# The last product of a decode layer turned from four rows into four columns, with the output stored from 128 partitions

## The chip, the cores and the metric

The kernel runs on one core of a Trainium2 chip, as one launch. The metric is the device time of one execution in microseconds; the kernel before takes 355.39 us, the median of three runs (355.38 to 355.53). Engine names in the profile: PE is TensorE (PEld its weight loads), DVE is VectorE, ACT is ScalarE, POOL is GpSimd, SP is SyncE, which here only issues DMAs.

## The reference

One decode step of a conditioned transformer block, for a single token with D = 512. The condition c gives six vectors of 512 (shift, scale and gate for each half). The first half is attention with 32 query heads over 8 cached key and value heads of 32768 positions; the second half is a feed-forward layer with 1792 hidden units.

```python
mod = (_silu(c) @ w_mod).reshape(c.shape[0], 6, 1, -1)
sa, ca, ga, sb, cb, gb = (mod[:, i] for i in range(6))
h = _layernorm(x) * (1 + ca) + sa
x = x + ga * attention(h, k_cache, v_cache, wq, wo)      # 8 heads x 32768 x 128, keys and values
h = _layernorm(x) * (1 + cb) + sb
x = x + gb * (relu(h @ w1) @ w2)                          # 512 -> 1792 -> 512
```

Everything is bf16 in memory. The key and value caches are 64 MB each, and the weights some 16 MB; all of it is read once.

## The kernel before

**Loads.** All large loads are issued from SP in one fixed order (`stream`, L139 to L144; `load` and `need`, L96 to L151): w_mod, wq, then keys and values in pieces of 4 MB, then wo in four pieces, w1 in two and w2 in six. They go into a ring of five slots of 32 KB per partition (L74); a load waits until the slot that it takes is free. w2 is held as 14 rows of 512 per partition, so `w2_sb[p, ft, d]` is the weight from hidden unit 14p + ft to output d. Its six pieces hold ft = 0 to 3, 4 to 6, 7 to 9, 10 and 11, 12, and 13 (`W2P`, L51).

**Column form and row form.** A vector of 512 in column form lies on 128 partitions, four elements each: element 4p + ko at partition p, column ko. x, the modulation vectors (`modT_sb`) and the residual after attention (`x1T`) are held like that. In row form it lies on four partitions, 128 elements each. `expand` and `four_rows` (L323 to L337) turn columns into four rows: the column form is multiplied into a masked 128x128 tile on VectorE, and a matmul with `rowpick` sums it into four rows of PSUM. The kernel does this for the last gate in the setup (`gb_rows`, L340) and for the residual during the second layer norm (`meanwhile`, L698, and L707).

**Order.** In the setup a scheduler orders the instructions. From L599 on, TensorE and VectorE run their instructions as written: for each of 8 heads keys are turned on VectorE (L405), scores are made on TensorE (L422), then softmax and the value product (L484). After the last head the tail is serial: the rest of the output projection (`project`, L555, of which the last two pieces use wo as the stationary operand and one column as the moving one, L567), gate and residual (L691, L692), the second layer norm (L250 to L280), the w1 product (L714), Relu and the w2 product. `keep_clock(n)` (L592) issues n matmuls whose result nobody reads, in places where TensorE would otherwise have nothing to do.

**The end of the tail.** The hidden vector is transposed on VectorE in two halves (L724), and ScalarE writes its Relu into `hid_bd`, a tile of 14 x 4 x 4 columns that was zeroed in the setup and of which only the diagonal of each 4x4 block is written. So the stationary operand `hid_bd[:, ft, i, :]` has one column that is not zero, column i, and the product with 128 columns of w2 adds to row i of a 4x128 tile in PSUM. There are 14 x 4 = 56 such matmuls (L735). Two VectorE operations on 4 partitions apply gate and residual (L740, L742), and SP stores four runs of 256 bytes (L743).

PSUM tiles that go by `bank` (L240) rotate over three banks; a new one takes the bank that was used three before.

Of the kernel before, what the change touches and what calls it, by code (L numbers as in the profile page):

```python
# [9 lines left out]
BF16 = mybir.dt.bfloat16  # L10
F32 = mybir.dt.float32
ACT = mybir.ActivationFunctionType
ALU = mybir.AluOpType
AX = mybir.AxisListType
# [3 lines left out]
def kernel(  # L18
# [14 lines left out]
    nc = tc.nc  # L33
    P = 128
# [4 lines left out]
    KT = D // P  # L39
    Dff = B_w1.shape[1]  # L40
    FT = Dff // P
# [33 lines left out]
    const = ctx.enter_context(tc.tile_pool(name="const", bufs=1))  # L75
# [85 lines left out]
    ident_f = const.tile([P, P], F32)  # L161
# [7 lines left out]
    for hp in range(4):  # L169
# [10 lines left out]
        out=mask4, in_=ident_f[:].rearrange("p (x q) -> p q x", q=REP), op=ALU.add, axis=AX.X,  # L180
# [3 lines left out]
    for n in sorted({n * REP for _, n in WOP}):  # L184
        cmask[n] = const.tile([P, P // n], F32, name=f"cmask{n}")
        nc.vector.tensor_reduce(
            out=cmask[n][:], in_=ident_f[:].rearrange("p (c r) -> p c r", r=n), op=ALU.add, axis=AX.X,
# [3 lines left out]
            out=rsel_f[:], in_=ident_f[:].rearrange("p (c r) -> p r c", r=n), op=ALU.add, axis=AX.X,  # L191
# [13 lines left out]
    place32 = const.tile([P, 32], F32)  # L205
    nc.vector.tensor_reduce(
        out=place32[:], in_=ident_f[:].rearrange("p (j m) -> p m j", m=32), op=ALU.add, axis=AX.X,
    )
    rowpick = const.tile([P, KT], F32)
    nc.vector.tensor_reduce(  # L210
        out=rowpick[:], in_=ident_f[:].rearrange("p (j m) -> p j m", m=32), op=ALU.add, axis=AX.X,
    )
    hid_bd = const.tile([P, FT, KT, KT], BF16)
    nc.gpsimd.memset(hid_bd[:], 0.0)

    pick8 = const.tile([16, 8], BF16)
    nc.vector.tensor_tensor(out=pick8[:], in0=ident_bf[0:16, 0:8], in1=ident_bf[0:16, 8:16], op=ALU.add)
# [22 lines left out]
    def bank(name):  # L240
        return ps_s.tile([P, 512], F32, tag="s", name=name)[:]
# [75 lines left out]
    for i in range(2):  # L317
# [1 line left out]
            mod_rows[:, i, :].rearrange("q (m ko) -> q ko m", ko=KT),  # L319
            modT_sb[:, 4 * KT * i:4 * KT * (i + 1)].rearrange("p (j ko) -> p j ko", j=4),  # L320
        )

    def expand(src_T, name):  # L323
        e = const.tile([P, 32, KT], F32, name=f"{name}_exp")
        nc.vector.tensor_tensor(
            out=e[:], in0=src_T.unsqueeze(1).to_broadcast([P, 32, KT]),
            in1=place32[:].unsqueeze(2).to_broadcast([P, 32, KT]), op=ALU.mult,
        )
        return e

    def four_rows(e, name):

        r_ps = bank(f"{name}_ps")[0:KT, 0:P]
        nc.tensor.matmul(  # L334
            r_ps, lhsT=rowpick[:], rhs=e[:].rearrange("p m kt -> p (m kt)"), start=True, stop=True,
        )
        return r_ps  # L337

    gb_rows = const.tile([KT, P], F32)
    nc.scalar.copy(out=gb_rows[:], in_=four_rows(expand(modT_sb[:, 5 * KT:6 * KT], "gb"), "gb"))  # L340

    hT = const.tile([P, KT], BF16)
    stat1 = const.tile([P, 2], F32)
# [5 lines left out]
    ncb = const.tile([P, KT], F32)  # L349
# [242 lines left out]
    def keep_clock(n):  # L592

        if not spare:
            spare.append(bank("spare_ps"))
        for _ in range(n):
            nc.tensor.matmul(spare[0], lhsT=ident_bf[:], rhs=qbd[0][:, :, 0:P], start=True, stop=True)  # L597

    with tc.manual_schedule(engines={mybir.EngineType.PE, mybir.EngineType.DVE}):  # L599
        build_qbd(0)  # L600
        for u in range(NTILE):
            for half in range(2):
                turn_k(0, u, half)
                scores(0, u, half)
            if u % 2 == 1:
                bank_max(0, u // 2)
        soft = softmax(0)
        for _ in soft:
            pass
        soft = None  # L610
        for g in range(LAST):
            h = g + 1
            build_qbd(h)
            turn_k(h, 0, 0)
            turn_k(h, 0, 1)
            turn_k(h, 1, 0)
            scores(h, 0, 0)
            if soft:
                next(soft)
            open_o(g)  # L620
            scores(h, 0, 1)
            if soft:
                next(soft)
            if g > 0:
                blocks(g - 1)
            scores(h, 1, 0)
            if g > 0:
                o_cols(g - 1)
            turn_k(h, 1, 1)
            scores(h, 1, 1)  # L630
            if soft:
                next(soft)
            if g > 0:
                normalise(g - 1)
                if g in [sum(w) for w in WOP]:
                    spread(part_of(g - 1))
            if soft:
                next(soft)
            bank_max(h, 0)
            next(soft or iter(()), None)  # L640
            pv(g, (0, 1))
            for u in (2, 3):
                for half in range(2):
                    turn_k(h, u, half)
                    scores(h, u, half)
            bank_max(h, 1)
            soft = softmax(h)
            next(soft)
            if g < LOOPED:
                pv(g, (2, 3))  # L650
                next(soft)
                continue
            next(soft)
            next(soft)
            pv(g, (2,), range(6))
            next(soft)
            next(soft)
            open_o(LAST)
            pv(g, (2,), range(6, 16))
            pv(g, (3,))  # L660
            next(soft)
            next(soft, None)
            a_rows.append(row_bank("a_ps"))
            blocks(g)
        pv(LAST, (0, 1))
        o_cols(LAST - 1)
        normalise(LAST - 1)
        pv(LAST, (2,))
        spread(2)
        hid_ps = ps_o.tile([P, 512], F32, tag="o", name="hid_ps")  # L670
        nc.vector.memset(hid_ps[:], 0.0)
        pv(LAST, (3,))
        blocks(LAST)
        project(0)
        keep_clock(2)
        o_cols(LAST)
        keep_clock(2)
        project(1)
        normalise(LAST)
        spread(3)  # L680
        keep_clock(2)
        project(2)
        keep_clock(1)
        join_rows()
        keep_clock(2)
        project(3)


        stat2 = const.tile([P, 2], F32)
        x1T = const.tile([P, KT], F32)  # L690
        nc.vector.tensor_tensor(out=x1T[:], in0=attnT_ps, in1=modT_sb[:, 2 * KT:3 * KT], op=ALU.mult)  # L691
        nc.vector.scalar_tensor_tensor(  # L692
            out=x1T[:], in0=x1T[:], scalar=1.0, in1=xT, op0=ALU.mult, op1=ALU.add, accum_out=stat2[:, 0:1],
        )
        h2T = const.tile([P, KT], BF16)
        x1_ps = []

        def meanwhile():  # L698
            e = expand(x1T[:], "x1")
            keep_clock(2)  # L700
            x1_ps.append(four_rows(e, "x1"))
            keep_clock(2)

        keep_clock(3)
        layernorm_T(x1T[:], stat2, h2T[:], modT_sb[:, 3 * KT:4 * KT], ncb[:], "ln2", meanwhile)
        x1_rows = const.tile([KT, P], F32)
        nc.vector.tensor_copy(out=x1_rows[:], in_=x1_ps[0])  # L707

        NQ = 32 * FT
        for part, (k0, k1) in enumerate(W1P):  # L710
            w1_sb = need(("w1", part))
            for kt in range(k0, k1):
                for q in range(4):
                    nc.tensor.matmul(  # L714
                        hid_ps[32 * q:32 * q + 1, 0:NQ], lhsT=h2T[:, kt:kt + 1],
                        rhs=w1_sb[:, kt - k0, q * NQ:(q + 1) * NQ], start=False, stop=(kt == KT - 1),
                        skip_group_check=True,
                    )
        keep_clock(3)
        hidT = rows_sb("hidT").rearrange("p a b -> p (a b)")[:, 0:NQ].rearrange("p (f e) -> p f e", e=32)  # L720
        hid_v = hid_ps[:, 0:NQ].rearrange("p (e f) -> p f e", f=FT)
        hb = hid_bd[:]
        for f0, f1 in ((0, FT // 2), (FT // 2, FT)):
            nc.vector.transpose(out=hidT[:, f0:f1], in_=hid_v[:, f0:f1])  # L724
            nc.scalar.activation(
                out=AP(hb.tensor, hb.offset + KT * KT * f0, [hb.ap[0], [KT * KT, f1 - f0], [KT + 1, KT]]),
                in_=hidT[:, f0:f1, 0:1].to_broadcast([P, f1 - f0, KT]), func=ACT.Relu,
            )

        ffn_ps = bank("ffn_ps")[0:KT, 0:P]  # L730
        for part, (f0, f1) in enumerate(W2P):
            w2_sb = need(("w2", part))
            for ft in range(f0, f1):
                for i in range(KT):
                    nc.tensor.matmul(  # L735
                        ffn_ps, lhsT=hid_bd[:, ft, i, :], rhs=w2_sb[:, ft - f0, i * P:(i + 1) * P],
                        start=(ft == 0 and i == 0), stop=(ft == FT - 1 and i == KT - 1),
                    )
        o_rows = const.tile([KT, P], F32)
        nc.vector.tensor_tensor(out=o_rows[:], in0=ffn_ps, in1=gb_rows[:], op=ALU.mult)  # L740
        o_bf = const.tile([KT, P], BF16)
        nc.vector.tensor_tensor(out=o_bf[:], in0=o_rows[:], in1=x1_rows[:], op=ALU.add)  # L742
    nc.sync.dma_start(out=out[0, 0].rearrange("(i n) -> i n", i=KT), in_=o_bf[:])  # L743


# [28 lines left out]
```

## Time and profile before

| what | value |
|---|---|
| median of three runs | 355.39 us |
| the profiled execution's own time | 355.74 us |
| its span, first to last instruction | 353.9 us |
| TensorE busy | 279.8 us, 79% of the span |
| VectorE busy | 203.1 us, 57% |
| HBM read | 149.42 MB, 422 GB/s over the span |
| DMA packets | 6852, of which 824 under 512 B |
| mean granted TensorE clock | 0.947 |
| w1 product (L714) | starts at 346.09 us |
| w2 product (L735), 56 matmuls | 347.89 to 351.18 us |
| issue of the store (L743) | 351.84 us |

Times inside the execution are microseconds from the start of the span. A row of the timeline merges instructions of one kind: start, length, engine, line, operation, output and inputs with their shapes, how many (x), and in square brackets how long the engine was idle before and what ended it. "128*4 128x128" in a matmul row is the stationary operand's shape and the moving operand's. Matmuls and weight loads overlap in the engine's pipeline, so the duration of one (a mean in ns) is longer than the distance from one to the next; the distance comes from the length of a merged row and its count.

### The profile page before, as it was taken

The page shows a single profiled execution, that of the slowest core. Times are in us where ns is not written, and L with a number is a line of the kernel's source. Part 1 is how long each engine was busy: PE and PEld are TensorE (multiplying, and loading weights), DVE is VectorE, ACT ScalarE, POOL GpSimd, SP SyncE. Part 2 cuts the span into 40 slices and gives each one's busy share as a digit, 9 for nine tenths or more (in the row PEclk, how much of TensorE's full clock was granted, in tenths as well). Part 3 has the DMA queues.
Part 4 walks back from the last instruction along what each step waited for, and adds up shares of the span by engine and source line. Part 5 has one row for each costly group of instructions (what it writes and reads, how often), then busy time and mean ns, then how long its engine had stood idle before and what let it go on. Part 6 is the DMA issues. An engine that isn't in the chain of part 4 may idle for free. (4 is left out here: it accounts for less than half of the span.)

```text
span 353.9 us, 4006 instructions
## 1 busy us (share of the span) xinstructions
PE 279.8 (79%) x1311; PEld 112.7 (32%) x1311; DVE 203.1 (57%) x271; ACT 25.4 (7%) x69; POOL 3.9 (1%) x16
## 2 busy tenths in 40 slices
PE   0542781999898979897979796979689687989996
PEld 0221230333343323332323232323234233334444
DVE  6245775882768268462939178553938095734142
ACT  1220003000010001000100001000100010002000
POOL 4000000000000000000000000000000000000000
PEclk9995997799899999998999899999999997999999
DMA  8999999999999999999999999999999999999994
GB/s 309 455 422 445 431 422 441 441 418 424 459 418 422 459 418 424 441 437 426 433 444 417 430 456 419 427 446 426 422 448 430 422 439 441 422 430 424 421 420 177
DMA packets 6852, 149.59 MB, mean 423 GB/s; under 512 B 824, under 2 KB 1080, under 8 KB 1976
## 3 DMA queue, kind: packets, MB, share of 16 engines
q1 hardware_dynamic: 6776, 149.43, 98.4%
q8 instruction: 8, 0.13, 0.1%
q14 instruction: 4, 0.03, 0.0%
q0 software_dynamic: 64, 0.00, 0.0%
HBM read 149.42 MB, written 0.00 MB: 422 GB/s over the span
## 5 line engine op out<-in xcount | busy, mean ns | idle before, releaser
L405 DVE STREAM_TRANSPOSE Ksb<-Ksb 128x2048 f32<-128x2048 f32 x64 | 142.9, 2281 | 63.9 <-DMA Ksb<-in_A_k_cache_dram 63.9
L484 PE MATMUL o_ps<-Vsb,PT_g 128*16 (+1 forms) x512 | 130.0, 395 | 21.5 <-ACT qbd L389 7.2
L422 PE MATMUL S_ps<-Ksb,qbd 128*128 128x512 bf16 x512 | 121.8, 388 | 23.5 <-DVE Ksb L405 21.9
L422 PEld LDWEIGHTS <-qbd 128*128 128x128 bf16 x512 | 49.0, 98 | 87.6 <-issue 31.8
L484 PEld LDWEIGHTS o_ps<-Vsb,PT_g 128*16 x416 | 37.4, 90 | 90.2 <-issue 63.7
L428 DVE TENSOR_SCALAR_CACHE_REDUCE S_g<-S_ps 128x512 f32<-128x512 f32 x16 | 11.0, 690 | 34.4 <-PE S_ps L422 34.4
L389 ACT COPY qbd<-qrep_sb 32x16 bf16<-32x16 bf16 x32 | 6.4, 201 | 138.7 <-PE S_ps L422 137.6
L465 DVE STREAM_TRANSPOSE PT_g<-P_g 128x1024 bf16<-128x1024 bf16 x8 | 9.7, 1218 | 6.6 <-ACT P_g L459 6.6
L484 PEld LDWEIGHTS <-PT_g 128*16 128x16 bf16 x96 | 8.2, 90 | 11.0
L456 ACT ACTIVATE nbias<-Mb_ps 128x1 f32<-128x1 f32 x8 | 1.4, 171 | 136.8 <-PE Mb_ps L454 136.8
L459 ACT ACTIVATE P_g<-S_g,nbias 128x1024 bf16<-128x1024 f32 x8 | 9.2, 1148 | 0.2
L227 PE MATMUL xc_ps<-cx_sel,cx_bd 16*128 16x2 bf16 x4 | 0.3, 172 | 11.1 <-DVE cx_bd L221 11.1
L515 DVE SCALAR_TENSOR_TENSOR Y<-o_ps,smask,Y 16x128 f32<-16x128 f32 x24 | 8.1, 339 | 0.8
L471 PE MATMUL L_ps<-Lexp,ones_f 128*128 128x4 f32 x16 | 3.0, 257 | 4.3 <-DVE Lexp L468 4.3
L597 PE MATMUL spare_ps<-qbd,ident_bf 128*128 128x512 bf16 x19 | 5.6, 380 | 0.0
L440 PE MATMUL mT_ps<-ident_f,m_p 128*1 128x128 f32 x8 | 2.2, 270 | 3.9 <-DVE m_p L437 2.0
L471 PEld LDWEIGHTS L_ps<-Lexp,ones_f 128*128 128x128 f32 x16 | 3.1, 221 | 5.8 <-issue 5.1
L443 DVE TENSOR_REDUCE Mrow<-mT_ps 1x4 f32<-1x128 f32 x8 | 2.1, 257 | 4.6 <-PE mT_ps L440 4.6
L534 DVE TENSOR_TENSOR oT_sb<-acc_ps,Linv 128x4 bf16<-128x4 f32 x8 | 1.2, 150 | 5.7 <-PE acc_ps L521 5.7
L295 PE MATMUL mod_ps<-wm_sb,siluT 128*1 128x512 bf16 x24 | 3.6, 624 | 1.0 <-DVE siluT L289 1.0
L505 DVE MEMSET o_ps<- 16x512 f32 x8 | 3.9, 485 | 0.8
L552 DVE CAST o_sb<-o_ps 128x4 bf16<-128x4 f32 (+2 forms) x4 | 0.7, 167 | 5.7 <-PE o_ps L548 5.7
(115 smaller groups left out, 80.0 us busy)
## 6 DMA issues: line engine op xcount, KB each, us to landing
Ksb<-in_A_k_cache_dram SPq DMA_DIRECT2D x16, 4096.0 KB, 35.6
Vsb<-in_A_v_cache_dram SPq DMA_DIRECT2D x15, 4096.0 KB, 35.2
wq_sb<-in_A_wq_dram SPq DMA_DIRECT2D x1, 4096.0 KB, 19.6
Vsb<-in_A_v_cache_dram SPq DMA_DIRECT2D x2, 2048.0 KB, 31.8
wm_sb<-in_w_mod_dram SPq DMA_DIRECT2D x1, 3072.0 KB, 10.4
wo_sb<-in_A_wo_dram SPq DMA_DIRECT2D x1, 2048.0 KB, 29.1
w_sb<-in_B_w_dram SPq DMA_DIRECT2D x1, 1344.0 KB
wo_sb<-in_A_wo_dram SPq DMA_DIRECT2D x1, 1024.0 KB, 31.1
```

The lines of the kernel that those rows point to most:

```text
L295: nc.tensor.matmul(dst[j // 4][32 * (j % 4):32 * (j % 4) + 1, :], lhsT=src_T[:, kt:kt + 1], rhs=w[:, kt, j * 512:(j + 1) * 512], start=(kt ...
L389: nc.scalar.copy(out=o, in_=i)
L405: t = nc.vector.transpose(out=KTt.bitcast(F32), in_=KTt.bitcast(F32))
L422: nc.tensor.matmul(S_ps_tiles[g], lhsT=qbd[g % 2][:, hp, 4 * (7 - s):4 * (7 - s) + P], rhs=KTv[:, 16 * sl:16 * sl + 16, h, :, par], start= ...
L428: nc.vector.tensor_scalar(out=S_tiles[g][:, G, :], in0=S_ps_tiles[g], scalar1=1.0, scalar2=None, op0=ALU.mult, op1=ALU.max, accum_out=m_ti ...
L459: nc.scalar.activation(out=P_g[:], in_=S_g[:].rearrange("p g f -> p (g f)"), func=ACT.Exp, bias=nbias[:], scale=scale, accum_out=l_g[:],)
L465: nc.vector.transpose(out=PT_g[:], in_=P_g[:])
L471: nc.tensor.matmul(L_ps[:], lhsT=ones_f[:], rhs=Lexp[:], start=True, stop=True)
L484: nc.tensor.matmul(o_tiles[g][:], lhsT=PT, rhs=Vx, start=False, stop=False, skip_group_check=True)
L505: nc.vector.memset(o_tiles[g][:], 0.0)
L515: nc.vector.scalar_tensor_tensor(out=Y[:], in0=o[:, s], scalar=smask[:, s:s + 1], in1=Y[:], op0=ALU.mult, op1=ALU.add,)
L597: nc.tensor.matmul(spare[0], lhsT=ident_bf[:], rhs=qbd[0][:, :, 0:P], start=True, stop=True)
```

## The change

The hidden vector now becomes the moving operand, one column per ft, and w2 the stationary one: for each ft and each ko a 128x128 piece of w2, taken with a step of four elements, is loaded as weights, and the product is added to column ko of a 128x4 tile in PSUM. That is again 56 matmuls. The PSUM tile is zeroed by VectorE ahead of them, and the matmuls only add. Relu writes a tile of 14 columns. Gate and residual are applied to columns, with `modT_sb` and `x1T` as they are, and the store takes eight bytes from each of 128 partitions. `rowpick`, `hid_bd`, `expand`, `four_rows`, `gb_rows` and `x1_rows` go, and the layer norm's `meanwhile` issues five spare matmuls instead of four and the transposing one.

```diff
-    rowpick = const.tile([P, KT], F32)
-    nc.vector.tensor_reduce(
-        out=rowpick[:], in_=ident_f[:].rearrange("p (j m) -> p j m", m=32), op=ALU.add, axis=AX.X,
-    )
-    hid_bd = const.tile([P, FT, KT, KT], BF16)
-    nc.gpsimd.memset(hid_bd[:], 0.0)
...
-    def expand(src_T, name):
...
-    def four_rows(e, name):
...
-    gb_rows = const.tile([KT, P], F32)
-    nc.scalar.copy(out=gb_rows[:], in_=four_rows(expand(modT_sb[:, 5 * KT:6 * KT], "gb"), "gb"))
...
-        x1_ps = []
-
-        def meanwhile():
-            e = expand(x1T[:], "x1")
-            keep_clock(2)
-            x1_ps.append(four_rows(e, "x1"))
-            keep_clock(2)
-
         keep_clock(3)
-        layernorm_T(x1T[:], stat2, h2T[:], modT_sb[:, 3 * KT:4 * KT], ncb[:], "ln2", meanwhile)
-        x1_rows = const.tile([KT, P], F32)
-        nc.vector.tensor_copy(out=x1_rows[:], in_=x1_ps[0])
+        layernorm_T(x1T[:], stat2, h2T[:], modT_sb[:, 3 * KT:4 * KT], ncb[:], "ln2", lambda: keep_clock(5))
+        ffn_ps = bank("ffn_ps")[:, 0:KT]
+        nc.vector.memset(ffn_ps, 0.0)
+        hid = const.tile([P, FT], BF16)
...
-        hb = hid_bd[:]
         for f0, f1 in ((0, FT // 2), (FT // 2, FT)):
             nc.vector.transpose(out=hidT[:, f0:f1], in_=hid_v[:, f0:f1])
-            nc.scalar.activation(
-                out=AP(hb.tensor, hb.offset + KT * KT * f0, [hb.ap[0], [KT * KT, f1 - f0], [KT + 1, KT]]),
-                in_=hidT[:, f0:f1, 0:1].to_broadcast([P, f1 - f0, KT]), func=ACT.Relu,
-            )
-
-        ffn_ps = bank("ffn_ps")[0:KT, 0:P]
+            nc.scalar.activation(out=hid[:, f0:f1], in_=hidT[:, f0:f1, 0], func=ACT.Relu)
+
         for part, (f0, f1) in enumerate(W2P):
             w2_sb = need(("w2", part))
             for ft in range(f0, f1):
-                for i in range(KT):
+                for ko in range(KT):
                     nc.tensor.matmul(
-                        ffn_ps, lhsT=hid_bd[:, ft, i, :], rhs=w2_sb[:, ft - f0, i * P:(i + 1) * P],
-                        start=(ft == 0 and i == 0), stop=(ft == FT - 1 and i == KT - 1),
+                        ffn_ps[:, ko:ko + 1], lhsT=w2_sb[:, ft - f0, :].rearrange("p (m ko) -> p ko m", ko=KT)[:, ko, :],
+                        rhs=hid[:, ft:ft + 1], start=False, stop=(ft == FT - 1), skip_group_check=True,
                     )
-        o_rows = const.tile([KT, P], F32)
-        nc.vector.tensor_tensor(out=o_rows[:], in0=ffn_ps, in1=gb_rows[:], op=ALU.mult)
-        o_bf = const.tile([KT, P], BF16)
-        nc.vector.tensor_tensor(out=o_bf[:], in0=o_rows[:], in1=x1_rows[:], op=ALU.add)
-    nc.sync.dma_start(out=out[0, 0].rearrange("(i n) -> i n", i=KT), in_=o_bf[:])
+        o_T = const.tile([P, KT], F32)
+        nc.vector.tensor_tensor(out=o_T[:], in0=ffn_ps, in1=modT_sb[:, 5 * KT:6 * KT], op=ALU.mult)
+        o_bf = const.tile([P, KT], BF16)
+        nc.vector.tensor_tensor(out=o_bf[:], in0=o_T[:], in1=x1T[:], op=ALU.add)
+    nc.sync.dma_start(out=out[0, 0].rearrange("(p k) -> p k", k=KT), in_=o_bf[:])
```

More of the change, by code (lines that the diff above doesn't have):

```diff
@@ L321 @@
         )
-    def expand(src_T, name):
[L324 to L327, printed above, removed]
-        )
-        return e
-    def four_rows(e, name):
[L333 to L337, printed above, removed]
-    gb_rows = const.tile([KT, P], F32)
-    nc.scalar.copy(out=gb_rows[:], in_=four_rows(expand(modT_sb[:, 5 * KT:6 * KT], "gb"), "gb"))
     hT = const.tile([P, KT], BF16)
@@ L721 @@
         hid_v = hid_ps[:, 0:NQ].rearrange("p (e f) -> p f e", f=FT)
-        hb = hid_bd[:]
         for f0, f1 in ((0, FT // 2), (FT // 2, FT)):
             nc.vector.transpose(out=hidT[:, f0:f1], in_=hid_v[:, f0:f1])
-            nc.scalar.activation(
-                out=AP(hb.tensor, hb.offset + KT * KT * f0, [hb.ap[0], [KT * KT, f1 - f0], [KT + 1, KT]]),
-                in_=hidT[:, f0:f1, 0:1].to_broadcast([P, f1 - f0, KT]), func=ACT.Relu,
-            )
-        ffn_ps = bank("ffn_ps")[0:KT, 0:P]
+            nc.scalar.activation(out=hid[:, f0:f1], in_=hidT[:, f0:f1, 0], func=ACT.Relu)
         for part, (f0, f1) in enumerate(W2P):
```

## The prediction

> **What bounds the kernel now.** I read the page's slices first, then the timeline of the last 14 us, the DMA issues with their landings, and the end of SP's queue. The slices:
>
> ```profile
> PE   0542781999898979897979796979689687989996
> ...
> DMA  8999999999999999999999999999999999999994
> ```
>
> The DMA engines are full from the first slice to the middle of the last, so the loads land when their bytes have come through, whatever is saved in the setup; and TensorE is busy almost throughout from slice 7. The chain of waits runs through TensorE's scores and value products to its tail, so time can be won or lost only behind the last loads, which is where the change is. The timeline of that tail (start us, duration us, engine, line, xcount; in square brackets idle time before and what ended it):
>
> ```profile
> 342.87 0.79 PEld L567 LDWEIGHTS <-wo_sb 128*128 128x128 bf16 x16
> 343.09 0.67 PE L567 MATMUL acc_ps<-o_sb,wo_sb 128*128 128x1 bf16 x16
> ...
> 343.79 0.16 DVE L691 TENSOR_TENSOR x1T<-acc_ps,modT_sb 128x4 f32<-128x4 f32 x1 [1.63 <-PE acc_ps L567]
> 343.99 0.16 DVE L692 SCALAR_TENSOR_TENSOR x1T<-x1T,xc 128x4 f32<-128x4 f32 x1
> ...
> 347.07 0.71 DVE L724 STREAM_TRANSPOSE hidT<-hid_ps 128x224 f32<-128x224 f32 x2 [0.85 <-PE hid_ps L714]
> 347.58 0.50 ACT L725 ACTIVATE hid_bd<-hidT 128x28 bf16<-128x28 f32 x2 [2.00 <-DVE hidT L724]
> 347.89 3.10 PEld L735 LDWEIGHTS <-hid_bd 128*4 128x4 bf16 x56 [0.62 <-ACT hid_bd L725]
> 347.89 3.29 PE L735 MATMUL ffn_ps<-w_sb,hid_bd 128*4 128x128 bf16 x56
> 351.22 0.28 DVE L740 TENSOR_TENSOR o_rows<-ffn_ps,gb_rows 4x128 f32<-4x128 f32 x1 [3.44 <-PE ffn_ps L735]
> 351.53 0.28 DVE L742 TENSOR_TENSOR o_bf<-o_rows,x_rows 4x128 bf16<-4x128 f32 x1
> 351.84 0.35 SPq L743 DMA_DIRECT2D out_dram<-o_bf  x1
> ```
>
> The reader sees a serial end: transpose, Relu, 56 products, two vector operations, the store. L567 is the same form as the new product: a 128x128 stationary taken with a step of four elements, one column moving. Next the landings of the last weight pieces (KB, us from issue):
>
> ```profile
> w_sb<-in_B_w_dram SPq DMA_DIRECT2D x1, 384.0 KB, 12.4
> ...
> w_sb<-in_B_w_dram SPq DMA_DIRECT2D x1, 256.0 KB, 10.6
> ...
> w_sb<-in_B_w_dram SPq DMA_DIRECT2D x1, 128.0 KB, 9.7
> ...
> w_sb<-in_B_w_dram SPq DMA_DIRECT2D x1, 128.0 KB, 8.7
> ```
>
> They were issued at 336.86, 339.27, 340.52 and 341.81, so pieces 2 to 5 of w2 land at about 349.3, 349.9, 350.2 and 350.5; pieces 0 and 1 (327.09 + 20.2, 332.01 + 16.3) at 347.3 and 348.3. The last reading is the store (window; busy of each engine; clock, DMA share, GB/s), and SP's wait for it:
>
> ```profile
> 352.60:352.65 0.05, 0.00 (x0) 0.00 (x0) 0.00 (x0) 0.00 (x0) 0.00 (x0) 1.00 0.09 16
> 352.65:352.70 0.05, 0.00 (x0) 0.00 (x0) 0.00 (x0) 0.00 (x0) 0.00 (x0) 1.00 0.03 5
> ...
> SPq L769 <- DMA out_dram<-o_bf: 0.4, 1, 0.4
> ```
>
> Its 8 packets (4 of data, 4 of completion) move 0.76 us after the issue, within 0.1 us; SP is released 0.35 us later, at 353.05, and 0.85 us of closing follow to 353.9.
>
> **The change part by part.**
>
> *Setup.* Gone: a POOL memset (0.30 us), the rowpick reduction (0.27), gb_exp (0.29), its two-pass matmul (0.38) and an ACT copy (0.26); the q_ps memsets move forward on VectorE. Counted at nothing: VectorE then waits 2.30 us for cx_row, and the q product at 20.92 waits for wq's landing (0.52 us idle, ended by that DMA). If that cover were gone, it would still only move work that waits for the K loads. SP's queue loses and gains no load.
>
> *The second layer norm.* x1_exp (0.28), the x_ps matmul (0.31 on the chain) and the x_rows copy (0.27) go; one more spare matmul (about 0.25) and a four-column memset come. The memset's nearest row is that of acc_ps, 128x8, 0.07 us; it stands where the copy stood, in front of 0.85 us of VectorE idle time, so it delays nothing, and the product that needs it starts 1.8 us later. TensorE's five spares fit between 344.80 and 346.09, where h2T (to 346.03) sets the start of the w1 product. Sum 0. If the spares overran, each would cost 0.22 us at most.
>
> *Relu.* 7 elements per half instead of 28. Bounds: 0.17 us (L456, 128x1) and 0.22 (L370, 128x16) against 0.264; I take 0.20, and 0.05 less ahead of it, because its extra wait on POOL goes (0.09 us from the transpose's end to the ACTIVATE; other handovers take 0.04). The stationary is now w2, whose load needs no Relu. So the first product starts at about 347.77 (where the three spares end as well), 0.12 earlier.
>
> *The 56 products.* Before: 3.30 / 56 = 59 ns each. After, by L567: 0.79 / 16 = 49.5 ns between starts, though one weight load lasts 117 ns and one matmul 172. Without waits: last matmul start 347.77 + 55 x 0.0495 = 350.49, end 350.67, VectorE at 350.70. But the landings come close. Four steps per f make 0.20 us: f = 7 would start at 349.16 against a landing at 349.3, f = 10 at 349.9 against 349.9, f = 12 at 350.3 against 350.2, f = 13 at 350.5 against 350.5. With 0.05 for a handover, the last four loads start at 350.55; the last of them 0.15 later, and its matmul ends 0.22 after that (L567: 343.54 to 343.76), so VectorE starts at 350.95. I take this end, because the landings are read from this very stretch; gain 351.22 - 350.95 = 0.27, and up to 0.52 if the landings do not bind. In the kernel before, the piece for f = 13 was needed only at 350.95: 0.45 us of slack, which covered the load and is used up.
>
> *Gate and residual.* 4x128 becomes 128x4: from 0.31 us step to step (351.22, 351.53, 351.84) to 0.20 (L691 to L692), twice: 0.22 gained.
>
> *The store.* 128 runs of 8 B instead of 4 of 256 B. No row shows such a store. Loads over 128 partitions are issued in 0.33 us against 0.35 here, which gives the lower end, -0.02. The 8 packets took 0.12 x 0.05 x 16 = 0.10 engine-us; were all of it data, 24 ns each. I assume eight runs on each of 16 engines, seven more than the one run of each engine in use now: 7 x 24 ns = 0.17. The upper end is a full confirmation (0.35 us) for each of the seven, 2.45. I take 0.17, since the packets' own time is the nearer row: the 0.35 us of confirmation follows the last packet once. The Trainium skill, "DMA: Bandwidth & Descriptors", section Bandwidth, has about 10.5 ns per packet for small loads, an estimate of 7 x 10.5 = 0.07 us, by which the sum would be 0.1 us lower. SP has only the closing semaphores (to 352.6) behind the store; every engine's closing waits for it.
>
> *Sum.* -0.27 - 0.22 + 0.17 = -0.32 us. The profiled execution took 355.74 (span 353.9 and 1.84 around it), so 355.42; it lies 0.35 above the median of 355.39, hence 355.07, which I call 355.1.
>
> **The rivals.** A change under 0.2% (0.71 us) counts as no change here, about what a measurement of this kernel tells apart.
>
> B, nothing waits for w2 and the store is free: -0.52 - 0.22 - 0.02 = -0.76, so 354.6, faster by just over the bound. For it: in an execution whose loads end 0.3 us earlier the pieces would not bind. Against it: the landings, and that it needs every term at its end.
>
> C, the small writes are confirmed late, and the kernel is slower. Place: between the store's last packet and SP's release. At 0.35 us for each of seven more writes of an engine: -0.49 + 2.45 = +1.96, 357.35. It decides from 0.49 / 7 = 0.07 us per write (slower at all) and from 1.20 / 7 = 0.17 us (slower by over 0.2%). For it: release already takes longer than moving the data; the runs lie next to each other in DRAM, and different engines write neighbouring ones. Against it: only one confirmation is seen. The same page of the Trainium skill (Specifications) has read-modify-write for anything under 512 B; that would hold for 256 B too and gives no price here.
>
> D, the weight loads do not overlap: 56 x 0.117 = 6.55 us, TensorE done at 354.5, VectorE 3.2 later than now: 355.39 + 3.3 - 0.22 + 0.17 = 358.6. Against it: L567 with the same step, 49.5 ns, twice, with the DMA share at 1.01 and 1.03. The Trainium skill, "TensorE: Matmul & The Clock Gate", section LDWEIGHTS, gives columns / 1.2 ns, 107 ns for 128 columns, so an estimate of 6.0 us for 56 of them; L567's single duration of 117 ns is near it, its spacing is half.
>
> **How the numbers follow.** The forecast A (pieces bind in part, the store costs up to about 1 us) has 0.60; its own range goes from 355.39 - 0.70 = 354.7 to 355.39 - 0.49 + 1.0 = 355.9. B 0.17, C beyond 0.17 us per write 0.19, D 0.04. Faster 0.17, same 0.60, slower 0.19 + 0.04 = 0.23. The range takes in A and B down to 354.5, and above up to the edge of C, 356.1; nearly all of C and D, some 0.2, is left out.
>
> **What would show it.** ffn products about 50 ns apart from 347.8, with short gaps before f = 7 and f = 13 whose idle time ends with w_sb's DMA; VectorE's first operation near 350.95, the store's issue near 351.35; 136 more packets under 512 B (128 + 16 - 8); SP's wait for the store about 0.6 us. I am wrong if products are 100 ns apart, if they never wait for w_sb, or if the store's release comes over 1.5 us after its issue (1.2 now).

## The result, and the profile after

The changed kernel takes 356.78 us (median of six runs, 356.29 to 357.07) against 355.44 us for the kernel before in the same runs: a ratio of 1.0037, 95% interval 1.0025 to 1.0049. It is slower by 1.34 us, where 0.3 us faster was forecast, and its runs spread over 0.8 us, those of before over 0.15. The profiled execution took 356.42 us with a span of 354.6, among the faster ones.

The timeline of the changed kernel's tail, the residual first and then the product and what follows it:

```profile
342.50 0.16 DVE L666 TENSOR_TENSOR x1T<-acc_ps,modT_sb 128x4 f32<-128x4 f32 x1 [1.62 <-PE acc_ps L542]
...
347.10 0.62 PEld L698 LDWEIGHTS <-w_sb 128*128 128x128 bf16 x16 [0.63 <-DMA w_sb<-in_B_w_dram]
...
348.10 0.48 PEld L698 LDWEIGHTS <-w_sb 128*128 128x128 bf16 x12 [0.38 <-DMA w_sb<-in_B_w_dram]
...
349.04 1.49 PEld L698 LDWEIGHTS <-w_sb 128*128 128x128 bf16 x28 [0.47 <-DMA w_sb<-in_B_w_dram]
349.04 1.57 PE L698 MATMUL ffn_ps<-hid,w_sb 128*128 128x1 bf16 x28 [0.38 <-DMA w_sb<-in_B_w_dram]
350.65 0.16 DVE L703 TENSOR_TENSOR o_T<-ffn_ps,modT_sb 128x4 f32<-128x4 f32 x1 [3.68 <-PE ffn_ps L698]
350.85 0.16 DVE L705 TENSOR_TENSOR o_bf<-o_T,x1T 128x4 bf16<-128x4 f32 x1
351.04 0.35 SPq L706 DMA_DIRECT2D out_dram<-o_bf  x1
```

The product now stops for w2's pieces (the idle times in brackets end with w_sb's DMA), and the store is issued at 351.04 instead of 351.84. Not all of these 0.8 us are the change's own. Up to the residual the tails of the two kernels are the same, yet `x1T` starts at 342.50 here and at 343.79 in the profiled execution of before, which ran late: it took 355.74 us where its kernel's median is 355.39, and its last piece was issued 0.23 us later (341.81 against 341.58). The first two experiments below give a better pair. The chain of waits has changed accordingly (start us, length, what):

```profile
341.58 8.70 DMA w_sb<-in_B_w_dram
350.27 0.05 issue
350.32 0.31 PE ffn_ps L698 x4
...
350.65 0.17 DVE o_T L703
...
350.85 0.16 DVE o_bf L705
```

The last piece of w2 lands at 350.27, its four products take 0.31 us, then come the two vector operations. The rest is lost behind the store. Its packets in the changed kernel (window, length, five engines' busy time, clock, DMA share, GB/s), its landing (us from the issue), and SP's wait:

```profile
351.90:351.95 0.05, 0.00 (x0) 0.00 (x0) 0.00 (x0) 0.00 (x0) 0.00 (x0) 0.50 0.59 8
351.95:352.00 0.05, 0.00 (x0) 0.00 (x0) 0.00 (x0) 0.00 (x0) 0.00 (x0) 0.50 0.47 7
352.00:352.10 0.10, 0.00 (x0) 0.00 (x0) 0.00 (x0) 0.00 (x0) 0.00 (x0) 0.50 0.16 2
352.10:352.30 0.20, 0.00 (x0) 0.00 (x0) 0.00 (x0) 0.00 (x0) 0.00 (x0) 0.50 0.00 0
...
out_dram<-o_bf SPq DMA_DIRECT2D x1, 1.0 KB, 2.7
...
SPq L732 <- DMA out_dram<-o_bf: 1.9, 1, 1.9
```

All 144 packets have moved by 352.1, 1.06 us after the issue (0.86 before). But SP is released 2.7 us after the issue, where it was 1.2 before, and its wait is 1.9 us instead of 0.4. Nothing moves in the 1.6 us between. This text calls the time from the end of the last packet to SP's release the confirmation; the profile does not show what happens in it. The trace does keep the times at which the store's completions (one 4-byte packet each, 16 of them here, 4 before) reached its semaphore. Before, the four came 1.12 to 1.18 us after the issue. In the changed kernel five came by 1.32, as early as in the stores below that are not late, and the others one or two at a time until 2.68. The 1.5 us lost between the issue and the release, less the 0.8 by which the issue comes earlier, are the 0.7 us by which this execution is longer than the profiled one of before (356.42 - 355.74).

### The profile page after: what moved, and what is told of

Same layout as the page of the kernel before. It is cut to its first block, busy times and chain, and to the rows that moved or that the text cites. A ratio compares the mean times of both kernels' runs of the same rounds, so it can differ in the third digit from the quotient of the medians.

```text
span 354.6 us, 3992 instructions
## 1 busy us (share of the span) xinstructions
PE 279.2 (79%) x1308; PEld 111.5 (31%) x1308; DVE 201.6 (57%) x268; ACT 25.1 (7%) x68; POOL 3.7 (1%) x15
## 5 line engine op out<-in xcount | busy, mean ns | idle before, releaser
L337 PE MATMUL q_ps<-wq_sb,hT 128*1 128x512 bf16 x32 | 3.6, 627 | 2.4 <-DMA wq_sb<-in_A_wq_dram 2.4
```

Source lines behind the costliest of these rows:

```text
L337: nc.tensor.matmul(q_ps[i][32 * a:32 * a + 1, :].rearrange("o (h e) -> o h e", e=32), lhsT=hT[:, kt:kt + 1], rhs=wq_f[:, kt, i, a], start= ...
```

## Experiments

In the table and the text below, "release" is the time from the store's issue to SP's release: the landing that the DMA view gives, or, where it gives none, the distance to the first closing operation of SP that waits for it. Each release is read from one profiled execution, each time is the median of several. The variants of the changed kernel share this edit, which makes room for other shapes of the store (the tile's unwritten part is zero, so they do not store the layer's result):

```diff
+    o_bf = const.tile([P, 128], BF16)
+    nc.gpsimd.memset(o_bf[:], 0.0)
...
-        o_bf = const.tile([P, KT], BF16)
-        nc.vector.tensor_tensor(out=o_bf[:], in0=o_T[:], in1=x1T[:], op=ALU.add)
+        nc.vector.tensor_tensor(out=o_bf[:, 0:KT], in0=o_T[:], in1=x1T[:], op=ALU.add)
```

### Is it the store?

Theory S: the store costs the time. Rival T: the product or the setup does. One experiment takes the store back in the changed kernel, the other puts the new store into the kernel before.

```diff
e1_cols_store4, in the changed kernel
+    nc.sync.dma_start(out=out[0, 0].rearrange("(i n) -> i n", i=KT), in_=o_bf[0:KT, :])
e2_rows_store128, in the kernel before (o_bf a tile of 128x128, the result in its first four partitions)
+    nc.sync.dma_start(out=out[0, 0].rearrange("(p k) -> p k", k=KT), in_=o_bf[:, 0:KT])
```

> The changed kernel with one thing put back: the store takes four runs of 256 B from four partitions (of a tile in which the result fills only the first four columns, so the output's values are not the layer's; the store still waits for the last vector operation). Theory S (the 128 small writes are confirmed late, 2.7 us from issue to release against 1.2): release again 1.2 us after the issue, time about 354.9 us, faster than before by some 0.5 us. Rival T (the store is innocent, the time goes into the product that waits for w2's pieces, or into the setup): time stays at 356.3 to 357.1 us.

> The kernel before with one thing changed: the store takes eight bytes from each of 128 partitions (of a tile in which only four partitions hold the result, so the output's values are not the layer's). Theory S: the release comes about 2.7 us after the issue, time 355.4 + 1.5 = 356.9 us, with more spread from run to run than before. Rival T: 355.4 to 355.6 us, since product and setup are as before.

Measured: e1 355.01 us against 355.38 (ratio 0.9990, interval 0.9980 to 0.9999); e2 357.14 against 355.38 (1.0050, 1.0035 to 1.0066). The waits of SP, e1 first:

```profile
SPq L733 <- DMA out_dram<-o_bf: 0.4, 1, 0.4
```

```profile
SPq L770 <- DMA out_dram<-o_bf: 2.3, 1, 2.3
```

S holds, T falls. With four runs the changed kernel is 0.37 us faster than before; the eight-byte store alone makes the kernel before 1.76 us slower. The two add up to the change: -0.37 + 1.76 = 1.39, measured 1.34.

The same two runs show what the rest of the change is worth, since e2 has the product of the kernel before, e1 the changed one, and their last pieces of w2 were issued within 0.02 us of each other (341.59 and 341.57). The product, VectorE's first operation after it and the store's issue, and from the chain of waits what the product's second half waited for, in e2:

```profile
347.21 3.56 PE L737 MATMUL ffn_ps<-w_sb,hid_bd 128*4 128x128 bf16 x56 [0.23 <-DMA w_sb<-in_B_w_dram]
350.82 0.28 DVE L742 TENSOR_TENSOR o_rows<-ffn_ps,gb_rows 4x128 f32<-4x128 f32 x1 [3.82 <-PE ffn_ps L737]
351.51 0.35 SPq L744 DMA_DIRECT2D out_dram<-o_bf  x1
...
336.63 12.38 DMA w_sb<-in_B_w_dram
...
349.06 1.74 PE ffn_ps L737 x28
```

and in e1:

```profile
350.64 0.16 DVE L705 TENSOR_TENSOR o_T<-ffn_ps,modT_sb 128x4 f32<-128x4 f32 x1 [3.67 <-PE ffn_ps L700]
351.10 0.35 SPq L707 DMA_DIRECT2D out_dram<-o_bf  x1
```

So in an execution whose tail does not run late the product of the kernel before waits for w2 as well: its second half starts when the third piece has landed, at 349.01. The changed product gains 0.18 us (350.82 to 350.64). From there to the store's issue it takes 0.46 us instead of 0.69, a gain of 0.23 for gate and residual. Together that is 0.41, against 0.37 measured.

### What in the store is late?

The next runs alter the number of runs, their size, their distance in DRAM, and who writes them. S1: an engine's eight writes are confirmed in turn (this was rival C's mechanism). S2: eight bytes are late, whatever the number. S3: neighbouring writes wait for each other. S4: sixteen engines have more to confirm than four.

```diff
e3_cols_16x64
+    nc.sync.dma_start(out=out[0, 0].rearrange("(p k) -> p k", p=16), in_=o_bf[0:16, 0:32])
e4_cols_16x8
+    nc.sync.dma_start(out=out[0, 0, 0:64].rearrange("(p k) -> p k", p=16), in_=o_bf[0:16, 0:KT])
e5_cols_64x8
+    nc.sync.dma_start(out=out[0, 0, 0:256].rearrange("(p k) -> p k", p=64), in_=o_bf[0:64, 0:KT])
e6_cols_pitch512 (e9 and e10 below: P x 8 and P x 16 instead of P x 256)
+    scratch = nc.dram_tensor("scratch", (P, 256), BF16, kind="Internal").ap()
+    nc.sync.dma_start(out=scratch[:, 0:KT], in_=o_bf[:, 0:KT])
e7_cols_128x512 (o_bf of 256 columns)
+    nc.sync.dma_start(out=scratch, in_=o_bf[:])
```

> The changed kernel with the store from 16 partitions, 64 bytes each (output's values not the layer's). S1 (each engine's eight writes are confirmed one after another, 0.2 us each): one write per engine, so the release is as early as with four runs, 1.2 us after the issue, time about 354.9 us. S2 (a run below some size is confirmed late, whatever the number): release 2 us or more after the issue, time 355.8 us or more. S4 (sixteen engines instead of four have to confirm): something between, 355.1 to 355.5 us.

> The changed kernel storing eight bytes from 16 partitions only (the first 64 outputs; the other 448 are not written). Same run size as the change, one run per engine, neighbours in DRAM. S1 (an engine's eight writes are confirmed one after another): release as with four runs, 1.2 to 1.3 us after the issue, about 355.1 us. S2 (any eight-byte write is confirmed late): about 2.7 us, 356.5 to 357 us. S3 (writes to neighbouring bytes of DRAM wait for each other): eight runs fall into the same 64 bytes as in the change, so late too, 356 us or more.

> The changed kernel storing eight bytes from 64 partitions (the first 256 outputs; the rest is not written): four runs per engine, neighbours in DRAM. S1: half of the extra, release about 2.0 us after the issue, 355.7 to 355.9 us. S2 and S3: as late as with 128 runs, 356.5 to 357 us.

> The changed kernel storing its 128 runs of eight bytes into a DRAM scratch at a distance of 512 bytes from each other (the output itself is not written). S1 and S2: late as in the change, 356.5 to 357 us. S3: no two runs are neighbours, release about 1.3 us after the issue, 355.1 us.

> The changed kernel storing 128 runs of 512 bytes into a DRAM scratch (the output itself is not written; 64 KB instead of 1 KB). Eight runs per engine as in the change, but long ones. S1: late as in the change, release 2.7 us after the issue or later, 356.5 us or more. S2 and S3: only the data's own time more (64 KB at 420 GB/s, 0.15 us), 355.1 to 355.3 us.

| run | runs x bytes, distance | release us | time us | before us |
|---|---|---|---|---|
| e3 | 16 x 64, adjacent | 1.3 | 355.13 | 355.38 |
| e4 | 16 x 8, adjacent | 1.3 | 355.26 | 355.33 |
| e5 | 64 x 8, adjacent | 3.4 | 357.21 | 355.33 |
| e6 | 128 x 8, 512 bytes apart | 1.4 | 355.28 | 355.33 |
| e7 | 128 x 512, adjacent | 1.5 | 355.35 | 355.33 |

The landings that the DMA view gives for e5 and e6:

```profile
out_dram<-o_bf SPq DMA_DIRECT2D x1, 0.5 KB, 3.4
```

```profile
scratch<-o_bf SPq DMA_DIRECT2D x1, 1.0 KB, 1.4
```

e6 has the change's 128 writes of eight bytes, with the same 16 completions, and is early: S1 and S2 fall, and with them the mechanism that rival C gave. S4 is worth 0.1 us at most (e3 has 16 completions and is released after 1.3 us, e1 has four and is released after 1.2), even though e3's 355.13 us lie in the range expected of it. What is left is the neighbourhood in DRAM, S3, although S3 had e4 late and it is early.

### Neighbours: at what distance, from which engine?

The next guess was a unit of 64 bytes, with a conflict either between engines (S3a) or between successive writes of one engine (S3b).

```diff
e12_cols_perm
+    nc.sync.dma_start(out=AP(out.tensor, out.offset, [[KT, 32], [32 * KT, 4], [1, KT]]), in_=o_bf[:, 0:KT])
e11_cols_32x8
+    nc.sync.dma_start(out=out[0, 0, 0:128].rearrange("(p k) -> p k", p=32), in_=o_bf[0:32, 0:KT])
```

> The changed kernel storing the same 128 runs of eight bytes into the same 1 KB, but partition 4a + b goes to place 32b + a, so that neighbours in DRAM come from partitions four apart and a partition's own neighbours land 256 bytes away (the output is a permutation of the layer's). S3a (writes of different engines into the same 64 bytes wait for each other): late as in the change, 356.5 to 357.2 us. S3b (successive writes of one engine into the same 64 bytes wait for each other, and an engine has neighbouring partitions): release about 1.4 us after the issue, 355.2 us.

> The changed kernel storing its 128 runs of eight bytes into a DRAM scratch at a distance of 16 bytes (the output itself is not written). Four neighbouring partitions share 64 bytes. S3b: late, 356.5 us or more. S3a, if an engine has four neighbouring partitions: no 64 bytes have two engines, 355.2 us.

> The same at a distance of 32 bytes: two neighbouring partitions share 64 bytes. S3b with 64 bytes as the unit: one write waits instead of three, release about 0.5 us later than without, 355.7 to 356 us. S3b with 32 bytes as the unit, and S3a: 355.2 us.

> The changed kernel storing eight bytes from 32 partitions (the first 128 outputs, the rest is not written): two runs per engine, neighbours in DRAM. S3b: one write of each engine waits, 355.7 to 356 us. S3a: several engines share each 64 bytes, as with 64 runs (357.2 us), 356.5 us or more.

Measured, with 355.31 us for the kernel before: e12 357.64 (release 3.6, of which 0.65 is the issue, 0.35 in the change), e9 355.19 (1.4), e10 355.20 (1.4), e11 356.92 (3.2). e12 and e11 are late, as S3a had it. A distance of 16 bytes is enough to be early, although four runs then share 64 bytes. So writes of one engine into the same 64 bytes do not delay each other, and S3b with that unit falls, provided that an engine has neighbouring partitions; S3a, 64 bytes shared between engines, was still left. Four more runs asked for the memory, for a single engine, for 16-byte runs, and for a copy that stays on the chip.

```diff
f1_scratch_128x8
+    scratch = nc.dram_tensor("scratch", (P, 4), BF16, kind="Internal").ap()
+    nc.sync.dma_start(out=scratch[:, 0:KT], in_=o_bf[:, 0:KT])
f2_cols_31x8
+    nc.sync.dma_start(out=out[0, 0, 0:124].rearrange("(p k) -> p k", p=31), in_=o_bf[0:31, 0:KT])
f3_cols_64x16
+    nc.sync.dma_start(out=out[0, 0].rearrange("(p k) -> p k", p=64), in_=o_bf[0:64, 0:8])
f6_cols_sbuf (o_to is a second tile of 128x4)
+    nc.sync.dma_start(out=o_to[:], in_=o_bf[:, 0:KT])
```

> The changed kernel storing its 128 runs of eight bytes one after the other into a DRAM scratch of 1 KB instead of the output (the output itself is not written). All late stores so far went to the output tensor, and the early ones at 16, 32 and 512 bytes' distance to a scratch. If the place matters (M, the output tensor's memory): early, 355.2 us. If the pattern matters (S3a, several engines' small writes within the same 64 bytes): late as in the change, 356.5 to 357.2 us.

> The changed kernel storing eight bytes from 31 partitions into the output (the first 124 outputs, the rest is not written). 31 has no divisor up to 16 but 1, so if the engines are dealt out by divisors, one engine writes all 31 runs (32 packets instead of 48). S3a: no 64 bytes are written by two engines, so no late confirmation; 30 more packets of one engine at 10 to 25 ns each make 0.3 to 0.75 us, 355.4 to 355.9 us. Adjacency, run size or the output's memory alone as the cause: 356.9 us or more, as with 32 partitions.

> The changed kernel storing 16 bytes from each of 64 partitions into the output (values not the layer's): four runs per engine, neighbours in DRAM, together 64 bytes if an engine has four neighbouring partitions. S3a: no 64 bytes have two engines, early, 355.3 us (0.2 more if the issue takes 0.55 as with 64 runs of eight bytes). M, or neighbouring small runs as such: late, 356.5 to 357.3 us.

> The changed kernel copying its 128 runs of eight bytes into another tile on the chip instead of DRAM (the output itself is not written). If the delay is DRAM's confirmation of partial writes: no more than 1.4 us from issue to release, 355.2 us or less. If it is the DMA engines' own handling of eight-byte runs: late, 356.5 us or more.

Measured, with 355.30 for the kernel before: f1 356.45 (release 2.8), f2 357.10 (3.3), f3 355.56 (1.7, its issue took 0.55), f6 355.49 (1.7, issue 0.53). The landing of f1, and the packets of f2, whose count shows one completion for 31 runs:

```profile
scratch<-o_bf SPq DMA_DIRECT2D x1, 1.0 KB, 2.8
...
DMA packets 32, 0.00 MB, mean 0 GB/s; under 512 B 32, under 2 KB 32, under 8 KB 32
...
SPq L733 <- DMA out_dram<-o_bf: 2.5, 1, 2.5
```

So it is not the output's memory (f1 is late in a scratch), and one engine alone is late (f2): S3a falls too. Runs of 16 bytes are early (f3), as are runs of eight bytes 16 apart (e9). That points to a unit of 16 bytes. f6 is early too, at 355.49 us neither of the two times expected of it, with 0.18 us of its release in the longer issue; but on the chip each run goes to a partition of its own, so no two are neighbours, and f6 cannot say whether only DRAM confirms neighbours late. The last pair asked whether both halves must come from one engine.

```diff
g1_other_engine
+    nc.sync.dma_start(out=out[0, 0].rearrange("(j q k) -> q j k", q=16, k=KT), in_=o_bf[0:16, 0:64].rearrange("q (j k) -> q j k", j=8)[:, :, 0:KT])
g2_same_engine
+    nc.sync.dma_start(out=out[0, 0].rearrange("(q j k) -> q j k", q=16, k=KT), in_=o_bf[0:16, 0:64].rearrange("q (j k) -> q j k", j=8)[:, :, 0:KT])
```

> The changed kernel storing 128 runs of eight bytes over the output's 1 KB from 16 partitions, eight runs each (values not the layer's), so that each of the 16 engines has one partition; run j of partition q goes to place 16j + q, so the two halves of any 16 bytes come from different partitions. S3b16 (one engine's second write into the same 16 bytes waits for the first to be done in DRAM): early, release about 1.4 to 1.7 us after the issue, 355.2 to 355.6 us. S3c (any two writes into the same 16 bytes): late, 356.4 us or more.

> The same 128 runs from the same places on the chip, but run j of partition q goes to place 8q + j, so both halves of any 16 bytes come from one partition. S3b16 and S3c: late, 356.4 us or more. Early here would leave only the 128 source partitions or the dealing of the runs as the cause.

Measured, with 355.25 for the kernel before: g1 356.51 (release 2.6), g2 357.56 (3.3, its issue 0.71). The landing of g1:

```profile
out_dram<-o_bf SPq DMA_DIRECT2D x1, 1.0 KB, 2.6
```

Both are late. g1 has 16 partitions and 16 completions; if each partition has an engine of its own, S3b falls as well, and a store with pairs of writes into the same 16 bytes is late whether one engine makes them or two.

Three things stay open. First, e4: its 16 runs make eight pairs that share 16 bytes, and it is early all the same. It has the fewest pairs, and with 16 completions for 16 runs it is the only one of these stores with a single write per engine; f2 (15 pairs, one engine) and e11 (16 pairs, two writes per engine) are late, so either can be the reason. Second, a rival that no run separates from the shared 16 bytes: if the tensors start at a multiple of 16 bytes, half of the runs of every late store start eight bytes past such a multiple, and none of an early one do, but for e4's. Eight-byte runs at a distance of 16 that start at byte 8 would tell the two apart. Third, the size. From the end of the last packet to the release every early store took 0.33 to 0.40 us and every late one 1.5 to 2.3, the longest with 15 pairs (f2), while the change has 64 and took 1.66. It is not that all completions are late: in the late stores with 16 of them, four to ten came as early as in an early store, and the rest followed a few at a time. In e5 nine came 1.55 to 1.65 us after the issue and the others at 2.07, 2.50, 2.92 and 3.35, one or two each time, so some 0.42 apart. What they wait for was not found.

### A version with four column groups

In the kernel before, the hidden column can be the stationary operand as it is, if the four parts of w2 go to different partitions of PSUM.

```diff
-                        ffn_ps, lhsT=hid_bd[:, ft, i, :], rhs=w2_sb[:, ft - f0, i * P:(i + 1) * P],
-                        start=(ft == 0 and i == 0), stop=(ft == FT - 1 and i == KT - 1),
+                        ffn_ps[32 * i:32 * i + 1, :], lhsT=hid[:, ft:ft + 1], rhs=w2_sb[:, ft - f0, i * P:(i + 1) * P],
+                        start=False, stop=(ft == FT - 1), skip_group_check=True,
...
+    nc.sync.dma_start(out=out[0, 0].rearrange("(i n) -> i n", i=KT), in_=AP(ob.tensor, ob.offset, [[32 * ob.ap[0][0], KT], [1, P]]))
```

> A version of the kernel before: the hidden column is the stationary operand as it is (one column, no block diagonal), and the four 128-column parts of w2 go to PSUM partitions 0, 32, 64 and 96, so gate, residual and the store of four runs of 256 B come from those partitions. If the matmuls to different partitions overlap as in the w1 product, the last piece's landing at about 350.5 sets the end of the product, VectorE starts at about 350.9 instead of 351.22, and the time is 355.1 us, 0.3 us faster than before. If they do not overlap, 59 ns each as before: 355.3 to 355.4 us.

Measured: 355.59 us against 355.38 (ratio 1.0007, interval 0.9998 to 1.0016): no gain. The timeline shows where it went:

```profile
347.10 0.39 PE L732 MATMUL ffn_ps<-w_sb,hid 128*1 128x128 bf16 x16 [0.24 <-DMA w_sb<-in_B_w_dram]
347.99 0.34 PE L732 MATMUL ffn_ps<-w_sb,hid 128*1 128x128 bf16 x12 [0.50 <-DMA w_sb<-in_B_w_dram]
...
350.54 0.29 DVE L737 TENSOR_TENSOR o_rows<-ffn_ps,gb_rows 128x128 f32<-128x128 f32 x1 [3.67 <-PE ffn_ps L732]
...
351.19 0.65 SPq L741 DMA_DIRECT2D out_dram<-o_bf  x1
```

The matmuls overlap (16 in 0.39 us), and the loads set their end, as expected. But the store from partitions 32 apart takes 0.65 us to issue instead of 0.35, and SP is released 1.7 us after the issue instead of 1.2, which the expectation had left out. Up to the issue this version is 0.32 us ahead of e2 (351.19 against 351.51); the store takes back 0.5, which leaves 0.18 lost, against 0.21 measured.

## Why the prediction was wrong

**The store: wrong, and this alone turned the sign.** The step was "I take 0.17, since the packets' own time is the nearer row: the 0.35 us of confirmation follows the last packet once." The packets' time was about right: they spread over 0.25 us instead of 0.1. The confirmation was not: 1.6 us after the last packet instead of 0.35, with SP's release 2.7 us after the issue, past the 1.5 that the prediction had named as a sign of being wrong. The store cost 1.76 us (e2), ten times the term. The only row at hand was a store of four long runs, which could show nothing of how writes to neighbouring bytes are confirmed; the upper end of 2.45 held the value, and the choice between the ends was wrong.

**Rival C: right in place and sign, wrong in mechanism.** It put the loss between the last packet and SP's release, which is where it is, and 0.19 on it. Its price per queued write is refuted: e6 and e7 have as many writes, with the same 16 completions, and are released after 1.4 and 1.5 us. So it is luck that its 1.96 us comes near the measured 1.34. Its remark that the runs lie next to each other in DRAM was the better lead, and it put no price on that. In the Trainium skill, "DMA: Bandwidth & Descriptors", the Specifications have read-modify-write for every transfer below 512 B. No run here shows whether that happens, but small size alone does not cost what was lost: eight bytes are early at 16 bytes' distance (e9), late side by side (f1).

**The product: right in what sets its end, too large by half in its gain.** The forecast gain of 0.27 was 0.18 (e2 against e1). It was read off an execution of the kernel before whose tail ran late and whose product therefore waited for no piece of w2; in e2 that product starts 0.68 us earlier (347.21 against 347.89) and waits. The step of 49.5 ns per weight load was, if anything, too long (16 loads in 0.62 us), the pieces' landings set the end, and VectorE started 0.38 us after the last landing (350.27 to 350.65), where 0.45 was reckoned. Rival D (loads that do not overlap) is out: 56 loads of 0.117 us would take 6.55 us, and VectorE started 3.55 us after the first load (347.10 to 350.65), waits included. Rival B's first half, that nothing waits for w2, did not come about.

**Gate and residual: right.** Two steps took 0.39 us (350.65 to 351.04), 0.40 reckoned; the gain was 0.23 (e2 against e1), 0.22 reckoned.

**Setup and layer norm: counted at nothing, and nothing shows against it.** Without the store's term the sum was -0.49; e1, which has everything but the store, measured -0.37, and -0.49 lies within its interval of -0.04 to -0.71. The tails of e1 and e2 alone account for 0.41 of it.

**The packets:** 136 more under 512 B were forecast; the page shows it.

```profile
DMA packets 6988, 149.59 MB, mean 422 GB/s; under 512 B 960, under 2 KB 1216, under 8 KB 2112
```

960 against 824.

**The range** ended at 356.1, "up to the edge of C", which left out what happened. With an upper end of 2.45 that nothing in the trace excluded, the range should have reached into C.

## What to carry to other kernels

A last store has nothing behind it to hide in: judge its form by SP's wait for it, not by its bytes or packets, and measure it alone before building the work in front of it around it. Where a column form ends in runs of eight bytes side by side in DRAM, its gain on TensorE and VectorE (0.37 us here) can be smaller than the late confirmation (1.76 us in e2); runs of 16 bytes or more were early. A faster product gains only up to the landing of its last weights. And before a sum is read off one profiled execution, compare its time with the median of its kernel: here it was 0.35 us above, and its product waited for no weights, where that of e2 does.

## What the runs showed of the hardware

- Stores with pairs of eight-byte writes into the same 16 bytes of DRAM were released 2.6 to 3.6 us after the issue (the change, e2, f1, f2, e5, e11, e12, g1, g2), against 1.2 to 1.7 for runs of 16 bytes or more, for eight bytes at 16, 32 and 512 bytes' distance, and for a copy on the chip. Sixteen adjacent runs with 16 completions were the exception (e4, 1.3 us). Whether the shared 16 bytes or the start at eight bytes past a multiple of 16 does it, no run tells.
- In such a late store part of the completions came as early as elsewhere and the rest followed a few at a time, until 2.68 us in the change, and 0.42 us apart in e5.
- The issue of a store depends on its shape: 0.32 to 0.36 us for most, but 0.53 for the copy on the chip (f6), 0.55 for 64 partitions (e5, f3), 0.65 for partitions 32 apart (v1) or a permuted target (e12), and 0.71 for g2.
- Products with one stationary column that go to four partitions 32 apart overlap: 16 with 128 moving columns in 0.39 us (v1), 24 ns each, against 59 ns each in the kernel before.
